# A float32 MLP's first product by seven half-size block products in place of eight, on one Trainium2 core

## Chip, cores and metric

The kernel runs on one core of a Trainium2 chip. The metric is the device time of one execution in microseconds (us). Engines: PE is TensorE (matmuls), DVE VectorE, ACT ScalarE, POOL GpSimd, SP SyncE, which issues most DMAs.

## The reference

Attention without a softmax, a norm, and two MLPs over 2304 tokens of 512 features, in float32:

```python
kv = np.einsum('bhsd,bhse->bhde', k, v)              # 4 batches, 8 heads, 576 x 64
out = np.einsum('bhsd,bhde->bhse', q, kv)
rms = np.sqrt(np.mean(out * out, axis=-1, keepdims=True) + 1e-06)
x = heads_side_by_side(out / rms * g_norm)           # 2304 x 512
# first MLP, w_in 512 x 2048
h = np.maximum(x @ w_in, 0.0); x = h * h @ w_out
# second MLP: 4 experts, w1[e] 512 x 1024, p = domain_probs / their sum
for e in range(4):
    h = np.maximum(x @ w1[e], 0.0)
    out2 += p[:, e:e + 1] * (h @ w2[e])
```

## The kernel before

Every float32 operand of a product is split into a high part in TensorE's reduced float32 format (`F32R`) and the rest in the same format; a product is three matmuls, high x low, low x high, high x high, added up in one bank of PSUM. `split` (L100) makes the parts: a copy on ACT gives the high part, a subtraction on POOL the low one.

Tokens are cut into blocks `BLK`, four of 512 and one of 256 (blocks 0 to 4). The inner features of the first MLP (2048) and of the second one (4 x 1024) are cut into slices of 256: slices 0 to 7 belong to the first MLP, 8 to 23 to the second. The kernel is a list of units, each a name that `run` (L348) turns into a call:

- `f<s>.<j>.<c>` is `g1` (L262): the first product of slice s for token block j and one of two feature chunks of 128, 4 inner chunks x 3 terms = 12 matmuls (L277) into one bank. In the first MLP ACT then takes ReLU and square and `split` the result. In the second ACT takes the ReLU into the high part `hh` (L285) and DVE makes the low part `hl` (L286).
- `g<s>.<j>.<c>` is `g2a` (L291), the second product of the first MLP: 2 x 3 matmuls (L301) for each of four output chunks, added to the accumulator `acc` on DVE (L308). After slice 7 the sum is split into `xh` and `xl`, the tokens of the second MLP.
- `h<s>.<j>.<t>` is `g2b` (L313), the second product of the second MLP: 2 x 3 matmuls (L323) for each tile of 128 tokens, scaled by the expert's weight and added to `acc` on DVE (L333). After the last slice the tile is stored.
- `w` is `split_w` (L138): the next quarter of a slice's weights is split, and a later quarter loaded into one of two `raw` buffers (L113). The weights of the first MLP come as float64 and are narrowed by six operations on DVE (L119 to L133).
- `k`, `o`, `c`, `b` are the attention: k^T v, q times that, norms, transposes. `p` works out the expert weights.

The list `RAMP` mixes the attention with slices 0 and 1; `rest` (L61) makes the order after it by rule: for each slice and block both `f` units, then the second products of the block before it, then a `w`. Each engine works through its instructions in order; the framework puts them in order at build time by the list, and a unit waits for a free buffer. Buffers that the change touches: eight banks of PSUM (`ps`), `tmp` (8 buffers of 2 KB per partition), weights in threes (`wp`), `hh` and `hl` in twos (`hp`), `xh` and `xl` as one tile each (`xp`).

Of the kernel before, what the change touches and what calls it, by code (L numbers as in the profile page):

```python
# [10 lines left out]
F32 = mybir.dt.float32  # L11
# [7 lines left out]
P = 128  # L19
# [39 lines left out]


def rest():  # L61
    def second(s, j):
        if s < NS1:
            return [f"g{s}.{j}.{c}" for c in range(KD)]
        return [f"h{s}.{j}.{t}" for t in range(BLK[j][1] // P)]

    r, prev = [], (1, NB - 1)
    for s in range(2, NS):
        for j in range(NB):
            r += [f"f{s}.{j}.{fc}" for fc in range(FC)] + second(*prev) + ["w"]  # L70
            prev = (s, j)
    return r + second(*prev)
# [3 lines left out]
def fused_kernel(ctx, tc, kvm, kvt, qt, g2, probs, w64, w32, out):  # L76
# [61 lines left out]
    def split_w():  # L138
        i = w_next[0]
        w_next[0] += 1  # L140
        s, c = divmod(i, 4)
        if s >= NS:
            return
        if c == 0:
            w_t[s] = [
                wp.tile([P, k, n], F32R, tag=t, name=f"{t}{s}")
                for t, k, n in (("ah", KD, FS), ("al", KD, FS), ("bh", FC, DM), ("bl", FC, DM))
            ]
        hi, lo = w_t[s][c // 2 * 2 : c // 2 * 2 + 2]
# [11 lines left out]
        load_w(i + 2)  # L161

# [1 line left out]
    kv_in, q_in, tails, stage, st_t, po_t, att_mid = {}, {}, {}, [None], {}, {}, {}  # L164
# [84 lines left out]
    def att_b(t):  # L249
        xn = att_mid.pop(t)  # L250
        pt = ps.tile([P, KD, P], F32, tag="ps", name=f"pt{t}")
        for c in range(KD):
            nc.tensor.transpose(pt[:, c, :], xn[:, c * P : (c + 1) * P], ident)  # L253
        dst = slice(t * P, (t + 1) * P)
        xg = tmp.tile([P, KD, P], F32, tag="tmp", name=f"xg{t}")
        nc.scalar.activation(out=xg, in_=pt, func=AF.Copy, scale=g_sb)
        split(xh[:, :, dst], xl[:, :, dst], xg)

# [1 line left out]
    h_t, acc_t = {}, {}  # L260

    def g1(s, j, fc):  # L262
        t0, n = BLK[j]
        ah, al = w_t[s][:2]
        if fc == 0:
            hh = hp.tile([P, FC, 512], F32R, tag="hh", name=f"hh{s}_{j}")
            hl = hp.tile([P, FC, 512], F32R, tag="hl", name=f"hl{s}_{j}")
            h_t[s, j] = (hh, hl)
        hh, hl = h_t[s, j]
        pt = ps.tile([P, 512], F32, tag="ps", name=f"p1_{s}_{j}_{fc}")  # L270
        fs = slice(fc * P, (fc + 1) * P)
        ts = slice(t0, t0 + n)
        steps = [
            (w[:, k, fs], x[:, k, ts]) for k in range(KD) for w, x in ((al, xh), (ah, xl), (ah, xh))
        ]
        for i, (w, x) in enumerate(steps):
            nc.tensor.matmul(pt[:, :n], w, x, start=(i == 0), stop=(i == len(steps) - 1))  # L277
        if s < NS1:
            r = tmp.tile([P, 512], F32, tag="tmp", name=f"r{s}_{j}_{fc}")
            nc.scalar.activation(out=r[:, :n], in_=pt[:, :n], func=AF.Relu)  # L280
            sq = tmp.tile([P, 512], F32, tag="tmp", name=f"s{s}_{j}_{fc}")
            nc.scalar.activation(out=sq[:, :n], in_=r[:, :n], func=AF.Square)
            split(hh[:, fc, :n], hl[:, fc, :n], sq[:, :n])
        else:
            nc.scalar.activation(out=hh[:, fc, :n], in_=pt[:, :n], func=AF.Relu)  # L285
            nc.vector.scalar_tensor_tensor(  # L286
                out=hl[:, fc, :n], in0=pt[:, :n], scalar=0.0, in1=hh[:, fc, :n].bitcast(F32),
                op0=ALU.max, op1=ALU.subtract,
            )

    def g2a(s, j, c):  # L291
        t0, n = BLK[j]
        bh, bl = w_t[s][2:]
        hh, hl = h_t[s, j]
# [13 lines left out]
        nc.vector.tensor_tensor(out=a, in0=pt[:, :n], in1=a, op=ALU.add)  # L308
        if s == NS1 - 1:
            ts = slice(t0, t0 + n)  # L310
            split(xh[:, c, ts], xl[:, c, ts], a)

    def g2b(s, j, i4):  # L313
# [32 lines left out]
    unit = dict(k=att_kv, o=att_a, c=att_c, b=att_b, w=split_w, p=probs_p, f=g1, g=g2a, h=g2b)  # L346

# [76 lines left out]
```

## Time and profile before

| | us |
|---|---|
| median of 3 runs | 1267.77 (1266.41 to 1270.11) |
| profiled execution, span from first to last instruction | 1264.5 |
| PE busy | 1242.0 (98%) |
| DVE busy | 613.8 (49%) |
| ACT busy | 327.6 (26%) |
| POOL busy | 318.9 (25%) |

The page of the profile gives busy times over the whole span; of the profiled execution it has no time but the span. Stretches of the span, waits and the chain of work that ended last are read from the trace, in us from the span's start. A matmul is pipelined, so the length of one is not the distance from one to the next.

### The profile page before, as it was taken

How to read it: one execution, taken by the hardware profiler on the slowest of the kernel's cores; microseconds unless marked ns; L12 is line 12 of the kernel's file. 1: busy time of each engine (PE TensorE's matmuls, PEld its weight loads, DVE VectorE, ACT ScalarE, POOL GpSimd, SP SyncE). 2: the span in 40 equal slices, each digit the busy share in tenths (PEclk: the TensorE clock that was granted, in tenths of full speed). 3: DMA queues.
4: the chain of work that ended last, by engine and by line, in shares of the span. 5: the costliest groups of instructions: out<-in, count | busy, mean ns of one | idle time of the engine just before them, and what ended most of it. 6: DMA issues, size and time to landing. Idle time of an engine off the chain costs nothing.

```text
span 1264.5 us, 14555 instructions
## 1 busy us (share of the span) xinstructions
PE 1242.0 (98%) x5960; PEld 1043.9 (83%) x5960; DVE 613.8 (49%) x897; ACT 327.6 (26%) x596; POOL 318.9 (25%) x260
## 2 busy tenths in 40 slices
PE   7999979999999999999999999999999999999998
PEld 6888768888888888888888888888888888888887
DVE  6977897877222223444344443444334433444434
ACT  3564334433434452111111111111111111110110
POOL 3566565644533471100101101001001001010000
PEclk9999989999999999999999999999999999999999
DMA  7701222111000100100001001001001000000003
GB/s 298 244 25 52 82 84 67 51 51 42 9 17 18 34 17 17 34 10 25 29 6 34 17 17 34 17 17 34 17 17 34 11 23 30 4 17 1 1 34 117
DMA packets 22243, 53.40 MB, mean 42 GB/s; under 512 B 2721, under 2 KB 2721, under 8 KB 22177
## 3 DMA queue, kind: packets, MB, share of 16 engines
q1 hardware_dynamic: 21888, 52.44, 12.1%
q8 instruction: 47, 0.77, 0.2%
q14 instruction: 20, 0.16, 0.0%
q10 hardware_dynamic: 288, 0.04, 0.0%
HBM read 47.75 MB, written 4.72 MB: 41 GB/s over the span
## 4 chain that ended last, share of the span: by engine, by line
PE 91%; DVE 6%; POOL 1%; issue 1%; ACT 1%; DMA 0%; POOLq 0%; ACTq 0%; DVEq 0%
PE p L277 44%; PE p L323 31%; PE p L301 13%; DVE k L133 1%; DVE u L128 1%; DVE u L123 1%; PE pk L195 1%; PE po L210 1%; DVE k L127 1%; DVE u L119 1%; DVE acc L308 1%; PE pt L253 0%; DVE st L220 0%; DVE k L132 0%; DMA kvs<-in_kvm 0%
## 5 line engine op out<-in xcount | busy, mean ns | idle before, releaser
L277 PE MATMUL p<-xh,al 128*128 128x512 f32 (+1 forms) x960 | 353.4, 368 | 0.0
L277 PE MATMUL p<-xl,ah 128*128 128x512 f32 (+1 forms) x960 | 353.3, 368 | 0.0
L277 PE MATMUL p<-xh,ah 128*128 128x512 f32 (+1 forms) x960 | 353.1, 368 | 0.0
L333 DVE SCALAR_TENSOR_TENSOR acc<-p,p_sb,acc 128x512 f32<-128x512 f32 x270 | 202.7, 751 | 143.3 <-PE p L323 140.9
L286 DVE SCALAR_TENSOR_TENSOR hl<-p,hh 128x512 fp32r<-128x512 f32 (+1 forms) x160 | 102.0, 637 | 317.1 <-ACT hh L285 317.1
L285 ACT ACTIVATE hh<-p 128x512 fp32r<-128x512 f32 (+1 forms) x160 | 88.6, 554 | 616.5 <-PE p L277 616.5
L323 PE MATMUL p<-bl,hh 128*128 128x512 f32 x576 | 224.3, 389 | 0.0
L323 PE MATMUL p<-bh,hl 128*128 128x512 f32 x576 | 224.3, 389 | 0.0
L323 PE MATMUL p<-bh,hh 128*128 128x512 f32 x576 | 224.1, 389 | 0.0
L277 PEld LDWEIGHTS p<-xh,al 128*128 128x128 f32 x960 | 181.0, 188 | 31.0 <-PE po L210 0.2
L277 PEld LDWEIGHTS p<-xl,ah 128*128 128x128 f32 x960 | 181.0, 189 | 30.7 <-POOL xl L102 0.2
L277 PEld LDWEIGHTS p<-xh,ah 128*128 128x128 f32 x960 | 180.9, 188 | 30.0
L308 DVE TENSOR_TENSOR acc<-p,acc 128x512 f32<-128x512 f32 (+1 forms) x140 | 88.0, 632 | 128.0 <-PE p L301 127.6
L102 POOL TENSOR_TENSOR al<-raw,ah 128x512 fp32r<-128x512 f32 x32 | 40.8, 1297 | 427.3 <-ACT ah L101 427.3
L102 POOL TENSOR_TENSOR hl<-s,hh 128x512 fp32r<-128x512 f32 (+1 forms) x80 | 100.0, 1254 | 146.3 <-ACT hh L101 125.2
L301 PE MATMUL p<-hl,bh 128*128 128x512 f32 (+1 forms) x320 | 120.0, 375 | 8.2 <-POOL hl L102 8.2
L323 PEld LDWEIGHTS p<-bh,hh 128*128 128x128 f32 x576 | 108.1, 188 | 22.6
L323 PEld LDWEIGHTS p<-bl,hh 128*128 128x128 f32 x576 | 108.2, 188 | 22.0
L323 PEld LDWEIGHTS p<-bh,hl 128*128 128x128 f32 x576 | 108.2, 188 | 21.8
L301 PE MATMUL p<-hh,bl 128*128 128x512 f32 (+1 forms) x320 | 119.5, 374 | 2.0 <-ACT hh L101 1.9
L301 PE MATMUL p<-hh,bh 128*128 128x512 f32 (+1 forms) x320 | 119.1, 372 | 0.0
L280 ACT ACTIVATE r<-p 128x512 f32<-128x512 f32 (+1 forms) x80 | 44.0, 550 | 139.2 <-PE p L277 133.5
(62 smaller groups left out, 919.3 us busy)
## 6 DMA issues: line engine op xcount, KB each, us to landing
raw<-in_w SPq DMA_DIRECT2D x32, 512.0 KB, 3.8
raw<-in_w SPq DMA_DIRECT2D x64, 256.0 KB, 3.0
kvm<-in_kvm SPq DMA_DIRECT2D x10, 512.0 KB, 3.8
q<-in_qt SPq DMA_DIRECT2D x18, 256.0 KB, 4.5
out<-acc SPq DMA_DIRECT2D x18, 256.0 KB, 2.0
kvs<-in_kvm SPq DMA_DIRECT2D x6, 512.0 KB, 7.3
kvt<-in_kvt SPq DMA_DIRECT2D x4, 256.0 KB, 6.1
p_raw<-in_probs ACTq DMA_DIRECT2D x1, 36.0 KB, 5.1
```

What stands on the lines that cost most here:

```text
L102: nc.gpsimd.tensor_tensor(out=lo, in0=full, in1=hi.bitcast(F32), op=ALU.subtract)
L119: nc.vector.tensor_scalar(out=u, in0=high, scalar1=3, scalar2=0x3FFFFFF8, op0=ALU.logical_shift_left, op1=ALU.bitwise_and,)
L123: nc.vector.scalar_tensor_tensor(out=u, in0=high, scalar=0xC0000000, in1=u, op0=ALU.bitwise_and, op1=ALU.bitwise_or)
L127: nc.vector.tensor_scalar(out=k, in0=high, scalar1=0x7FFFFFFF, scalar2=None, op0=ALU.bitwise_and)
L277: nc.tensor.matmul(pt[:, :n], w, x, start=(i == 0), stop=(i == len(steps) - 1))
L280: nc.scalar.activation(out=r[:, :n], in_=pt[:, :n], func=AF.Relu)
L285: nc.scalar.activation(out=hh[:, fc, :n], in_=pt[:, :n], func=AF.Relu)
L286: nc.vector.scalar_tensor_tensor(out=hl[:, fc, :n], in0=pt[:, :n], scalar=0.0, in1=hh[:, fc, :n].bitcast(F32), op0=ALU.max, op1=ALU.subtract,)
L301: nc.tensor.matmul(pt[:, :n], w, h, start=(i == 0), stop=(i == len(steps) - 1))
L308: nc.vector.tensor_tensor(out=a, in0=pt[:, :n], in1=a, op=ALU.add)
L323: nc.tensor.matmul(pt, h, w, start=(i == 0), stop=(i == len(steps) - 1))
L333: nc.vector.scalar_tensor_tensor(out=a, in0=pt, scalar=pe, in1=a, op0=ALU.mult, op1=ALU.add)
```

## The change

In the second MLP the first product of two token blocks of 512 is taken as one product of 2 x 2 blocks: the weights of a slice, 512 x 256, are four blocks a11, a21, a12, a22 of 256 x 128, and the tokens four blocks b11 to b22 of 256 x 512. Seven block products and sums before and after them (Winograd's form of Strassen's algorithm) give what eight gave.

- Sums of weights: s1 to s4, on DVE (`operands`), once per slice; then splits of the four blocks and the four sums.
- Sums of tokens: t1 to t4, on DVE, for the pair (0, 1) ahead of the second MLP and for the pair (2, 3) ahead of the second group (units `x<g>.<i>`, function `right`). Four buffers `o` in the place of the x tiles hold the parts of all seven right operands: b11 and t2, t1 and t3, b21 and b22, t4.
- Products: units `s<v>.<b>.<i>`, i from 0 to 6, 6 matmuls each, into four banks a to d; products 4, 5 and 6 add into a bank that already holds a product. ACT copies one bank (p1), DVE adds u2, u4 and three more sums, and ReLU and `hl` follow as before.
- Two groups: all sixteen slices for blocks 0, 1 and 4, then all sixteen again for blocks 2 and 3. So the second MLP's weights are loaded and split twice; a pass of a slice has a number v, 8 to 39. Block 4 keeps its old products.
- Order: `merge` puts the second products of the blocks before between the seven products.
- Buffers: the x tiles by block, both parts of a weight in one tile, constants of the attention in its own pool, and a pool `ext` in the attention's place after `RAMP` with a third pair of h buffers and the second weight operand. A load of the second MLP's weights brings two quarters (512 KB).

```diff
+GRP2 = (((0, 1), (4,)), ((2, 3),))
 def rest():
...
+    for v in range(2, NS1):
         for j in range(NB):
...
+            if v == NS1 - 1 and j >= 2:
+                r += [f"x0.{j - 2}"]
+    for g, group in enumerate(GRP2):
+        for v in range(NS1 + g * NS2, NS1 + (g + 1) * NS2):
+            for blk in group:
+                b = blk[0]
+                if v == NS1 and b == 0:
+                    r += second(*prev) + ["x0.3"]
+                    prev = (v, ())
...
+                if v == NS1 + NS2:
+                    r += [f"x1.{i}" for i in range(4)]
+                if len(blk) == 2:
+                    units = [f"s{v}.{b}.{i}" for i in range(7)]
+                else:
+                    units = [f"f{v}.{b}.{fc}" for fc in range(FC)]
+                r += ["w"] * (blk == group[0]) + merge(units, second(*prev)) + ["w"] * (blk == group[-1])
+                prev = (v, blk)
...
+    def operands(i, v):
...
+        nc.vector.tensor_tensor(out=s1, in0=a21, in1=a22, op=ALU.add)
+        nc.vector.tensor_tensor(out=s2, in0=s1, in1=a11, op=ALU.subtract)
+        nc.vector.tensor_tensor(out=s3, in0=a11, in1=a21, op=ALU.subtract)
+        nc.vector.tensor_tensor(out=s4, in0=a12, in1=s2, op=ALU.subtract)
+        for n, a in enumerate(w_t[v]):
+            split(*(a[:, x, 0:2].rearrange("p o k f -> p (o k) f") for x in range(2)), r[:, :, n * P : (n + 1) * P])
+            split(*(a[:, x, 2:4] for x in range(2)), st[n])
...
+    OPS = (("b11", "t2"), ("t1", "t3"), ("b21", "b22"), ("t4",))
...
+        o = xp.tile([P, 2, 4, 512], F32R, tag="xs", name=f"o{g}_{i}", bufs=4)
+        for m, name in enumerate(OPS[i]):
+            o_t[pair[0], name] = (o, m * 2)
+            for k in range(2):
+                hi, lo = o[:, 0, m * 2 + k, :], o[:, 1, m * 2 + k, :]
+                if name[0] == "b":
+                    split(hi, lo, x_part(pair, name, k))
+                    continue
+                full = t_sum(pair, name, k)
+                nc.scalar.activation(out=hi, in_=full, func=AF.Copy)
+                nc.vector.tensor_tensor(out=lo, in0=full, in1=hi.bitcast(F32), op=ALU.subtract)
...
+    def t_sum(pair, name, k):
...
+        if name == "t3":
+            return sub("t3", b22, b12)
+        t1 = sub("t1", b12, b11)
+        if name == "t1":
+            return t1
+        t2 = sub("t2", b22, t1)
+        return t2 if name == "t2" else sub("t4", b21, t2)
...
+    PRODUCTS = (
+        (0, 0, "b11", "a", False), (0, 3, "t2", "b", False), (0, 2, "t1", "c", False),
+        (1, 2, "t3", "d", False), (1, 3, "b22", "c", True), (0, 1, "b21", "a", True),
+        (1, 1, "t4", "d", True),
+    )
...
+    def g1s(v, b, i):
...
+        steps = [
+            (w[:, x, op, k, :], o[:, y, k0 + k, :]) for k in range(2) for x, y in ((1, 0), (0, 1), (0, 0))
+        ]
...
+        if i == 0:
+            nc.scalar.activation(out=new("p1"), in_=pa, func=AF.Copy)
+        elif i == 1:
+            nc.vector.tensor_tensor(out=new("u2"), in0=pb, in1=su["p1"], op=ALU.add)
+        elif i == 2:
+            nc.vector.tensor_tensor(out=new("u4"), in0=pc, in1=su["u2"], op=ALU.add)
+        elif i == 3:
...
+            nc.vector.tensor_tensor(out=pb, in0=pd, in1=su["u4"], op=ALU.add)
+            relu(v, j2, 1, pb)
+        elif i == 4:
+            nc.vector.tensor_tensor(out=pc, in0=pc, in1=su["u2"], op=ALU.add)
+            relu(v, j2, 0, pc)
+        elif i == 5:
+            relu(v, j1, 0, pa)
+        else:
+            nc.vector.tensor_tensor(out=pd, in0=pd, in1=su["u2"], op=ALU.add)
+            relu(v, j1, 1, pd)
```

The order that `rest` gives, around the start of the second MLP, in a pass of the first group, and in one of the second:

```
f7.2.0 f7.2.1 g7.1.0 .. g7.1.3 x0.0 f7.3.0 f7.3.1 g7.2.0 .. g7.2.3 x0.1 f7.4.0 f7.4.1 g7.3.0 .. g7.3.3 x0.2
g7.4.0 .. g7.4.3 x0.3 w s8.0.0 .. s8.0.6 x0.4 f8.4.0 h8.1.0 .. h8.1.3 f8.4.1 h8.0.0 .. h8.0.3 w
w s9.0.0 s9.0.1 s9.0.2 s9.0.3 h8.4.0 s9.0.4 s9.0.5 s9.0.6 h8.4.1 f9.4.0 h9.1.0 .. h9.1.3 f9.4.1 h9.0.0 .. h9.0.3 w
w w s25.2.0 h24.3.0 s25.2.1 h24.3.1 s25.2.2 h24.3.2 s25.2.3 h24.3.3 s25.2.4 h24.2.0 s25.2.5 h24.2.1 s25.2.6 h24.2.2 h24.2.3
```

## Rows read from the trace of the kernel before

**Rows 1.** The page, busy us of each engine (share) and instructions.
```profile
PE 1242.0 (98%) x5960; PEld 1043.9 (83%) x5960; DVE 613.8 (49%) x897; ACT 327.6 (26%) x596; POOL 318.9 (25%) x260
```
**Rows 2.** Busy time by stretch; the header names the columns.
```profile
core 0: us, PE busy (x) PEld busy (x) DVE busy (x) ACT busy (x) POOL busy (x), PEclk, DMA share, GB/s
160.00:200.00 40.00, 34.99 (x155) 28.79 (x156) 39.62 (x47) 16.40 (x30) 27.37 (x21) 0.91 0.25 80
200.00:240.00 40.00, 40.00 (x201) 34.07 (x200) 31.95 (x43) 17.02 (x30) 22.18 (x17) 1.00 0.18 58
420.00:480.00 60.00, 60.00 (x300) 51.15 (x299) 16.96 (x29) 31.91 (x56) 38.51 (x34) 1.00 0.08 27
480.00:1260.00 780.00, 780.00 (x3622) 653.55 (x3621) 315.16 (x446) 117.49 (x214) 70.70 (x57) 1.00 0.07 23
```
**Rows 3.** Waits of PE in the whole span: us in total, times, longest.
```profile
PE p L301 <- POOL hl L102: 8.2, 5, 3.2
PE pk L195 <- DMA kvs<-in_kvm: 5.3, 2, 5.1
PE p L301 <- ACT hh L101: 1.9, 2, 1.3
```
**Rows 4.** Chain of work in the second MLP: start us, us, what, matmuls.
```profile
954.74 2.87 PE p L277 x24
957.61 5.47 PE p L323 x24
963.08 5.44 PE p L277 x24
...
976.68 5.44 PE p L323 x24
```
**Rows 5.** Groups by line and shape, PE: count | busy us, mean ns.
```profile
L277 PE MATMUL p<-xh,al 128*128 128x512 f32 x768 | 299.2, 390 | 0.0
L323 PE MATMUL p<-bl,hh 128*128 128x512 f32 x576 | 224.3, 389 | 0.0
```
**Rows 6.** Groups by line and shape, DVE, ACT, POOL; last, line 128's min/median/max.
```profile
L333 DVE SCALAR_TENSOR_TENSOR acc<-p,p_sb,acc 128x512 f32<-128x512 f32 x270 | 202.7, 751 | 143.3 <-PE p L323 140.9
L286 DVE SCALAR_TENSOR_TENSOR hl<-p,hh 128x512 fp32r<-128x512 f32 x128 | 88.5, 692 | 296.5 <-ACT hh L285 296.5
L285 ACT ACTIVATE hh<-p 128x512 fp32r<-128x512 f32 x128 | 76.5, 598 | 512.9 <-PE p L277 512.9
L308 DVE TENSOR_TENSOR acc<-p,acc 128x512 f32<-128x512 f32 x112 | 76.5, 686 | 107.1 <-PE p L301 106.9
L102 POOL TENSOR_TENSOR al<-raw,ah 128x512 fp32r<-128x512 f32 x32 | 40.8, 1297 | 427.3 <-ACT ah L101 427.3
L128 DVE SCALAR_TENSOR_TENSOR u<-k,u 128x512 f32<-128x512 uint32 x32 | 30.7, 959 | 0.3
L101 ACT ACTIVATE ah<-raw 128x512 fp32r<-128x512 f32 x32 | 18.5, 624 | 14.3 <-PE p L277 14.2
L286 DVE SCALAR_TENSOR_TENSOR hl<-p,hh 128x256 fp32r<-128x256 f32 x32 | 13.5, 420 | 20.6 <-ACT hh L285 20.6
L308 DVE TENSOR_TENSOR acc<-p,acc 128x256 f32<-128x256 f32 x28 | 11.5, 419 | 20.8 <-PE p L301 20.8
...
L128 DVE SCALAR_TENSOR_TENSOR u<-k,u x32: 674/693/1693, 11.2 to 314.7; 128x512 f32<-128x512 uint32 x32
```
**Rows 7.** DVE and POOL in order of time: start us, us, engine, line.
```profile
293.50 0.68 DVE L128 SCALAR_TENSOR_TENSOR u<-k,u 128x512 f32<-128x512 uint32 x1
294.10 0.68 DVE L308 TENSOR_TENSOR acc<-p,acc 128x512 f32<-128x512 f32 x1
294.70 0.41 DVE L132 TENSOR_SCALAR k<-u 128x512 uint32<-128x512 uint32 x1
...
301.13 1.69 DVE L128 SCALAR_TENSOR_TENSOR u<-k,u 128x512 f32<-128x512 uint32 x1
...
300.98 1.30 POOL L102 TENSOR_TENSOR hl<-s,hh 128x512 fp32r<-128x512 f32 x1 [1.43 <-ACT hh L101]
```
**Rows 8.** DMA issues of the page: count, KB each, median us to landing.
```profile
raw<-in_w SPq DMA_DIRECT2D x32, 512.0 KB, 3.8
raw<-in_w SPq DMA_DIRECT2D x64, 256.0 KB, 3.0
...
out<-acc SPq DMA_DIRECT2D x18, 256.0 KB, 2.0
```
**Rows 9.** DVE in order of time, its last instruction.
```profile
1260.67 0.75 DVE L333 SCALAR_TENSOR_TENSOR acc<-p,p_sb,acc 128x512 f32<-128x512 f32 x1 [0.61 <-PE p L323]
```

More of the change, by code (lines that the diff above doesn't have):

```diff
@@ L253, in att_b @@
             nc.tensor.transpose(pt[:, c, :], xn[:, c * P : (c + 1) * P], ident)
-        dst = slice(t * P, (t + 1) * P)
+        x = x_t[t // 4]
+        dst = slice(t % 4 * P, (t % 4 + 1) * P)
         xg = tmp.tile([P, KD, P], F32, tag="tmp", name=f"xg{t}")
         nc.scalar.activation(out=xg, in_=pt, func=AF.Copy, scale=g_sb)
-        split(xh[:, :, dst], xl[:, :, dst], xg)
+        split(x[:, 0, :, dst], x[:, 1, :, dst], xg)
     h_t, acc_t = {}, {}
-    def g1(s, j, fc):
[L263 to L269, printed above, removed]
-        pt = ps.tile([P, 512], F32, tag="ps", name=f"p1_{s}_{j}_{fc}")
[L271 to L275, printed above, removed]
+    n_h = [0]
@@ new lines, in new_h, with left @@
+    def new_h(v, j):
+        pool, more = (ext, "3") if ext is not None and n_h[0] % 3 == 2 else (hp, "")
+        n_h[0] += 1
+        h_t[v, j] = [
+            pool.tile([P, FC, 512], F32R, tag=t + more, name=f"{t}{v}_{j}") for t in ("hh", "hl")
+        ]
+        return h_t[v, j]
+    def g1(s, j, fc):
+        n = BLK[j][1]
+        x = x_t[j]
+        hh, hl = new_h(s, j) if fc == 0 else h_t[s, j]
+        pt = ps.tile([P, 512], F32, tag="ps", name=f"p1_{s}_{j}_{fc}")
+        def left(part, k):
+            if s < NS1:
+                return w_t[s][0][:, part, k, fc * P : (fc + 1) * P]
+            return w_t[s][fc][:, part, k // 2, k % 2, :]
+        steps = [(left(a, k), x[:, b, k, :]) for k in range(KD) for a, b in ((1, 0), (0, 1), (0, 0))]
@@ L276, in g1 @@
         for i, (w, x) in enumerate(steps):
             nc.tensor.matmul(pt[:, :n], w, x, start=(i == 0), stop=(i == len(steps) - 1))
[L278 to L289, printed above, removed]
+        if s >= NS1:
+            relu(s, j, fc, pt[:, :n])
+            return
@@ L308, in g2a, with x_part, right @@
         nc.vector.tensor_tensor(out=a, in0=pt[:, :n], in1=a, op=ALU.add)
[L309 to L313, printed above, removed]
+    OPS = (("b11", "t2"), ("t1", "t3"), ("b21", "b22"), ("t4",))
+    PLACE = {n: (i, k) for i, names in enumerate(OPS) for k, n in enumerate(names)}
+    o_t, t_tmp = {}, {}
+    def x_part(pair, name, k):
+        return acc_t[pair[int(name[2]) - 1]][:, (int(name[1]) - 1) * 2 + k, :]
+    def right(g, i):
+        pair, *alone = GRP2[g]
+        if i == 4:
+            (j,) = alone[0]
+            x_t[j] = xp.tile([P, 2, KD, BLK[j][1]], F32R, tag="xt", name=f"xb{j}", bufs=1)
+            for k in range(0, KD, 2):
+                split(*(x_t[j][:, a, k : k + 2, :] for a in range(2)), acc_t[j][:, k : k + 2, :])
+            return
+        o = xp.tile([P, 2, 4, 512], F32R, tag="xs", name=f"o{g}_{i}", bufs=4)
[9 more added lines that the diff above has]
+                nc.vector.tensor_tensor(out=lo, in0=full, in1=hi.bitcast(F32), op=ALU.subtract)
@@ new lines, in t_sum, with sub @@
+    def t_sum(pair, name, k):
+        b11, b12, b21, b22 = (x_part(pair, f"b{x}", k) for x in ("11", "12", "21", "22"))
+        def sub(m, a, b):
+            t = tmp.tile([P, 512], F32, tag="tmp", name=f"{m}_{name}_{pair[0]}_{k}")
+            nc.vector.tensor_tensor(out=t, in0=a, in1=b, op=ALU.subtract)
+            return t
+        if name == "t3":
[5 more added lines that the diff above has]
+        return t2 if name == "t2" else sub("t4", b21, t2)
@@ new lines, in fused_kernel, with new @@
+    PRODUCTS = (
+        (0, 0, "b11", "a", False), (0, 3, "t2", "b", False), (0, 2, "t1", "c", False),
+        (1, 2, "t3", "d", False), (1, 3, "b22", "c", True), (0, 1, "b21", "a", True),
+        (1, 1, "t4", "d", True),
+    )
+    pr, su = {}, {}
+    def g1s(v, b, i):
+        j1, j2 = b, b + 1
+        place, op, name, bank, more = PRODUCTS[i]
+        w = w_t[v][place]
+        o, k0 = o_t[b, name]
+        if not more:
+            pr[bank] = ps.tile([P, 512], F32, tag="ps", name=f"p{bank}{v}_{b}")
+        steps = [
+            (w[:, x, op, k, :], o[:, y, k0 + k, :]) for k in range(2) for x, y in ((1, 0), (0, 1), (0, 0))
+        ]
+        for m, (x, y) in enumerate(steps):
+            nc.tensor.matmul(
+                pr[bank], x, y, start=(m == 0 and not more), stop=(m == len(steps) - 1),
+                skip_group_check=more,
+            )
+        pa, pb, pc, pd = (pr.get(x) for x in "abcd")
+        def new(m):
+            su[m] = tmp.tile([P, 512], F32, tag="tmp", name=f"{m}_{v}_{b}")
+            return su[m]
+        if i == 0:
[5 more added lines that the diff above has]
+        elif i == 3:
+            new_h(v, j2)
+            new_h(v, j1)
+            nc.vector.tensor_tensor(out=pb, in0=pd, in1=su["u4"], op=ALU.add)
[5 more added lines that the diff above has]
+            relu(v, j1, 0, pa)
+        else:
+            nc.vector.tensor_tensor(out=pd, in0=pd, in1=su["u2"], op=ALU.add)
+            relu(v, j1, 1, pd)
@@ L344, in probs_p @@
         )
-    unit = dict(k=att_kv, o=att_a, c=att_c, b=att_b, w=split_w, p=probs_p, f=g1, g=g2a, h=g2b)
+    unit = dict(
+        k=att_kv, o=att_a, c=att_c, b=att_b, w=split_w, p=probs_p, f=g1, g=g2a, x=right, s=g1s, h=g2b
+    )
+    ext = None
     def run(name):
@@ L353, in fused_kernel @@
         small = actx.enter_context(tc.tile_pool(name="small", bufs=3))
+        g_sb = small.tile([P, 1], F32, name="g_sb", bufs=1)
+        ident = small.tile([P, P], F32, name="ident", bufs=1)
+        kvd += [small.tile([P, P], F32, name=f"kvd{i}", bufs=1) for i in range(NKVD)]
         make_identity(nc, ident)
```

134 lines of the change are left out of this document (92 added, 42 removed).

## Prediction, made before the changed kernel was run

> **What bounds the kernel now.** I read the busy shares first, then the busy time by stretch, then the waits of TensorE (PE), then the chain of work. The shares put PE at 1242.0 of 1264.5 us and VectorE (DVE) at 613.8 [rows 1]; that is an average, so the stretches matter. From 200 us on PE is busy for the whole of each stretch, 780.00 of 780 us from 480 to 1260, while DVE is busy for 315.16, ScalarE (ACT) for 117.49 and GpSimd (POOL) for 70.70 of them, at a granted clock of 1.00, the 2.4 GHz level [rows 2]. PE idles 1264.5 - 1242.0 = 22.5 us; 3.8 of it is the end behind the last accumulation at 1260.67 [rows 9], and some 18.6 lie before 200 us, where PE's longest waits are for hl, for a k/v load and for hh [rows 3]. From 160 to 200 DVE is busy 39.62 of 40 us and PE only 34.99, at a clock of 0.91 [rows 2]: the start is held by DVE, the second MLP by PE alone.
>
> A busy PE can still be a slow one, so I take its rate from the chain: 24 matmuls of 512 columns take 5.44 us, 226.7 ns each, on line 277 as on line 323, and 24 of 256 columns 2.87 us, 119.6 ns each [rows 4]. The 390 ns in the groups by line [rows 5] is the length of one matmul, which overlaps the next; it must not be multiplied by a count. A slice of the second MLP is four blocks of 5.44 and one of 2.87 on line 277 and 4.5 of 5.44 on line 323, 49.1 us; sixteen slices are 786 us, the length of the stretch. So a matmul removed in the second MLP is worth 226.7 ns, as long as nothing else becomes late.
>
> **What the change removes.** Line 277 ran 96 matmuls of 512 columns per slice (4 blocks x 2 feature chunks x 4 inner chunks x 3 terms; 768 x 3 over 24 slices [rows 5]). A pair of blocks takes seven products of 2 x 3 = 6 now, 42 instead of 48. Two pairs, sixteen slices: 32 x 6 = 192 matmuls fewer, 192 x 226.7 ns = 43.5 us. Block 4 and the second products keep their counts. PE per slice becomes 9.52 + 2.87 + 60 x 0.2267 = 26.0 us in the first group (blocks 0, 1, 4) and 9.52 + 48 x 0.2267 = 20.4 us in the second, 46.4 for 49.1.
>
> The Trainium skill (TensorE: Matmul & The Clock Gate, Back-to-back issue gap) puts a sustained stream of weight load and matmul at about 131 ns for 512 columns; by it the 192 would be worth 25.2 us. The chain has 226.7 ns in every slice, so the rule does not hold here, and the sum goes by the row.
>
> **What it adds in the steady slices.** Per pair and slice DVE gets five adds of a bank and a buffer. Their nearest row is the add of line 308, 686 ns at 512 columns [rows 6]; back to back, the next operation starts 0.60 us after such a one [rows 7]. It also gets four sums of weights at 256 columns: 419 ns (line 308 at 256 [rows 6]), or that plus a wait for POOL (below). What stays is hl at 692 ns (420 for block 4) and the accumulation at 751 [rows 6]. First group, per 26.0 us of PE: 5 x 0.69 + 4 x 0.42 + 4 x 0.69 + 2 x 0.42 + 10 x 0.75 = 16.2 us, 62%. Second, per 20.4 us: 3.4 + 1.7 + 2.8 + 8 x 0.75 = 13.9 us, 68%. DVE was at 315 of 780, 40%; it still isn't full. ACT has one copy and six splits at 0.62 and four to six ReLUs at 0.60 per slice, POOL six splits at 1.30 = 7.8 us of 20.4 [rows 6]. Neither is near PE.
>
> What counts is one wait that is new: product 4 (counted from 0) adds into the bank of product 2, so its first matmul waits until DVE has read that bank for u4, and every matmul behind it in PE's queue waits too. Between the end of product 2 and the start of product 4 stand product 3 (1.36 us) and one second-product tile (1.36 us): 2.72 us for an add of 0.69, so DVE may be 2 us late at no cost. In the very first slice no tile stands there, and it is 1.36. Products 5 and 6 add into banks read two to four units earlier. A pair holds four banks; four are left for tiles that need one for 1.36 + 0.75 us. I count both at nothing; the cover is DVE's 32 to 38% of idle time.
>
> **The price that the trace shows beforehand: DVE against POOL.** Line 128 reads two buffers in SBUF; it takes 674 ns at best and 959 on average [rows 6], while POOL is busy a little over half of the time [rows 2]. At 301.13 one took 1.69 us: POOL had begun an operation of 1.30 at 300.98, and the DVE one ended 0.54 us after it; at 293.50, with POOL idle, it took 0.68 [rows 7]. So an operation on two buffers waits out POOL's, and all new sums of weights and of tokens are of that kind. At 512 columns such a sum costs 0.69 (no POOL) to 0.69 + 1.3; I take 0.69 + 0.27, from the mean of line 128. The Trainium skill (SBUF — State Buffer, Who interferes with whom) states it as an exclusive lock, held for a whole instruction, when DVE has two SBUF inputs; the trace agrees (1.69 against 0.68 us), and it speaks against putting these sums on DVE beside POOL's splits. In steady slices 4 x 0.27 = 1.1 us falls at the slice's start, ahead of u2 and u4, inside the 2 us above. I allow 0.8 us in all for slices where it doesn't fit; the bounds are 0 and 0.5 us in each of 32 pairs, 16 us.
>
> **The two changes of operands.** Before each group the token sums are made: on DVE 6 operations for t2, 4 each for t1 and t3, 8 for t4, 22 in all, 15.2 us (13.2 back to back); on ACT 14 copies, 8.8 us; on POOL 6 subtractions, 7.8 us.
> Change A, into the second MLP: the sums can start when block 1 is complete. PE still has f7.3, g7.2, f7.4, g7.3, g7.4 then: 3 x 5.44 + 2 x 2.87 = 22.1 us, and t4 is needed only 8.2 us after that. DVE owes 12 accumulations there (8 x 0.69 + 4 x 0.42 = 7.2 us), then three adds and a split: 22 + 3 = 25 us of 30, plus 22 x 0.27 = 6. Just full. Bounds 0 and 6 us; I take 1.
> Change B, between the groups: the four operand buffers come free one by one as the last pair of slice 23 runs. From its product 1 to product 3 of the next pair, PE has 27.4 us of work. DVE owes 15.1 + 1.2 of its own (all back to back: adds 3.1, hl 3.2, 11 accumulations 7.3, weights 1.5, the new u2 and u4 1.2) and 8.5 for t2, t1 and t3: 24.8 us, plus 18 waits for POOL of 0.27 = 5. That is 2 us over; t4 adds 4.9 in the next 5. Bounds 0 and 10 us; I take 3.
>
> **Edits at nothing.** The second MLP's weights are loaded and split twice: 64 loads of 512 KB at 3.8 us instead of 64 of 256 KB at 3.0 [rows 8], two per 20 to 26 us and a slice ahead. The first group's ten stores now stand in the middle of SP's queue, each behind its accumulation, with loads behind them; the slice of lead covers that. The end keeps its form: the last accumulation, then a store of 2.0 us [rows 8, 9]. The third h buffer and the x tiles by block only loosen waits; the order of the start may shift either way (bounds -3 and +3 around its 18.6 us); I take 0.
>
> **The rivals.**
> 1. Forecast. Span 1264.5 - 43.5 + 0.8 + 1 + 3 = 1225.8. The page gives no time of that execution but its span; the median of the runs, 1267.77, is 3.3 above it, so 1229. Own range 1221 (no stall, start 3 shorter) to 1237. For it: PE is full in all of the second MLP, and DVE keeps a third.
> 2. DVE against POOL decides at both changes and in some slices: 6 + 10 + 5 us given back, 1267.8 - 43.5 + 21 = 1245. For it: 1.69 against 0.68. Against: POOL's 7.8 us per slice leave most of it free.
> 3. Slower: product 4 waits for u4 in every pair. At 43.5 / 32 = 1.36 us per pair the gain is gone; that needs DVE 3.4 us late each time, as when all four weight sums wait out an operation of POOL (5.2 us) right in front of u2. All 5.2 late gives 3.2 us per pair, 1327; 2 us per pair, the middle of that case, gives 1288. Against: the sums run at a slice's start, three products earlier.
> 4. The removed matmuls are worth less than the spacing, since pairs run slower: 42 in 10.1 us instead of 9.52 gives back 18.3, 1247. Against: one rate on both lines, and a change of line costs 0.03 us (5.47 against 5.44 [rows 4]). This is the time that the page's 131 ns would give.
>
> **Chances.** Forecast 0.75, rival 2 0.15, rival 3 0.05 with another 0.03 at no change, rival 4 0.02. The range 1221 to 1246 takes in 1 and most of 2. A measurement of this kernel tells some 0.3% (3.8 us) from no change. Faster 0.92, within 0.3% 0.03, slower 0.05.
>
> **What would show it.** In the chain, 42 matmuls of 9.52 us per pair; PE busy throughout the second MLP but for gaps of 1 to 5 us at its first pair and between the groups; waits of PE for u4 under 5 us in sum; token sums near 0.96 us on average. Wrong, if PE waits for DVE in every slice, if a product takes more than 1.36 us, or if the first 200 us change by more than 3.

## The result, and the profile after

The changed kernel takes 1235.58 us (median of 4 runs, 1235.17 to 1238.97) against 1267.32: a ratio of 0.975, 95% interval 0.9732 to 0.9767, 31.7 us less. The prediction was 1229.0 us, 38.8 less than the 1267.77 known then, with a range of 1221 to 1246.

The page has PE still at 98%, busy for 35.5 us less, and DVE at 64% where it was at 49% [rows 1]. It also shows the loads of weights, to set beside [rows 8]:

```profile
PE 1206.5 (98%) x5768; PEld 1012.0 (82%) x5768; DVE 797.5 (64%) x1229; ACT 427.3 (35%) x766; POOL 486.0 (39%) x382
...
raw<-in_w SPq DMA_DIRECT2D x96, 512.0 KB, 3.7
```

Busy time by stretch, with the columns of [rows 2]. The stretches are the start, the first MLP, the change to the second one, the first group, the change between the groups, the second group:

```profile
core 0: us, PE busy (x) PEld busy (x) DVE busy (x) ACT busy (x) POOL busy (x), PEclk, DMA share, GB/s
0.00:200.00 200.00, 180.23 (x950) 151.47 (x951) 163.12 (x257) 89.53 (x172) 110.98 (x94) 0.97 0.37 127
200.00:460.00 260.00, 260.00 (x1261) 220.09 (x1260) 131.94 (x194) 106.56 (x185) 116.89 (x92) 1.00 0.11 35
460.00:500.00 40.00, 37.56 (x199) 32.04 (x198) 34.28 (x48) 18.76 (x38) 21.26 (x15) 1.00 0.04 14
500.00:870.00 370.00, 370.00 (x1790) 312.80 (x1789) 221.84 (x355) 102.07 (x184) 110.73 (x86) 1.00 0.12 42
870.00:930.00 60.00, 55.37 (x239) 44.71 (x238) 53.14 (x76) 22.90 (x41) 27.67 (x19) 0.94 0.23 79
930.00:1220.00 290.00, 290.00 (x1281) 240.15 (x1280) 184.61 (x292) 86.85 (x148) 98.50 (x76) 1.00 0.13 44
```

In both groups PE is busy for the whole of the stretch, 370.00 of 370 and 290.00 of 290 us, with DVE at 60 and 64%. In the chain a product of six matmuls takes 1.36 us, 226.7 ns each as in [rows 4], and product 4 (into bank c) follows its tile with no gap:

```profile
530.96 1.36 PE pa L467 x6
532.32 1.36 PE pb L467 x6
533.68 1.36 PE pc L467 x6
535.04 1.36 PE pd L467 x6
536.40 1.36 PE p L512 x6
537.76 1.36 PE pc L467 x6
```

What was lost lies at the two changes of operands. At the first, PE idles 40 - 37.56 = 2.4 us, at the second 60 - 55.37 = 4.6, and there the granted clock averages 0.94. In the stretches of 3 us further down it is 0.56, 0.50 and 0.80: with two levels, 1.00 and 0.50, that is 6.8 us at half speed, worth 3.4 us of matmuls at most. The profiled execution was also 3.4 us longer than the other three, for a reason at its start (below).

The second change in detail. PE in order of time (start us, us, engine, line, what was waited for):

```profile
895.36 1.52 PE L467 MATMUL pa<-o,a 128*128 128x512 f32 x6
...
899.44 1.48 PE L467 MATMUL pd<-o,a 128*128 128x512 f32 x4
901.64 0.73 PE L467 MATMUL pd<-o,a 128*128 128x512 f32 x2 [0.73 <-DVE o L429]
...
905.50 1.42 PE L467 MATMUL pa<-o,a 128*128 128x512 f32 x5 [1.75 <-ACT p L478]
908.95 2.93 PE L467 MATMUL pc<-o,a 128*128 128x512 f32 x6 [2.02 <-DVE u L482]
```

DVE beside it; line 437 makes token sums, 429 their low parts, 480 is u2, 482 is u4:

```profile
902.17 0.67 DVE L437 TENSOR_TENSOR t_t<-acc,acc 128x512 f32<-128x512 f32 x1
902.88 1.42 DVE L437 TENSOR_TENSOR t_t<-acc,t_t 128x512 f32<-128x512 f32 x2
904.22 0.69 DVE L437 TENSOR_TENSOR t_t<-acc,acc 128x512 f32<-128x512 f32 x1
905.01 0.69 DVE L437 TENSOR_TENSOR t_t<-acc,t_t 128x512 f32<-128x512 f32 x1
905.62 0.69 DVE L429 TENSOR_TENSOR o<-t_t,o 128x512 fp32r<-128x512 f32 x1
906.22 0.69 DVE L437 TENSOR_TENSOR t_t<-acc,t_t 128x512 f32<-128x512 f32 x1
906.82 0.69 DVE L480 TENSOR_TENSOR u<-pb,p 128x512 f32<-128x512 f32 x1
907.60 0.69 DVE L429 TENSOR_TENSOR o<-t_t,o 128x512 fp32r<-128x512 f32 x1
908.21 0.68 DVE L482 TENSOR_TENSOR u<-pc,u 128x512 f32<-128x512 f32 x1
```

And ACT, whose copy p1 (line 478) stands behind a copy for t4 that itself waits for DVE:

```profile
904.34 0.63 ACT L428 ACTIVATE o<-t_t 128x512 fp32r<-128x512 f32 x1 [7.18 <-DVE t_t L437]
904.87 0.58 ACT L478 ACTIVATE p<-pa 128x512 f32<-128x512 f32 x1
```

The operands of product 0 were ready in time. u4, which product 4 needs, is ready only at 908.9, because the operations for t4, which only product 6 needs, stand ahead: on DVE seven of the eight ahead of u2 and all eight ahead of u4, and on ACT t4's first copy ahead of p1. The gap of 1.75 us has the same cause: PE's order has five matmuls of product 5 ahead of product 4 here, and product 5 adds into bank a, so it waits until p1, the copy of that bank, is made. The 0.73 us at 901.64 are another matter: there product 3 waits for a low part of its own operand, t3. Right behind the two long gaps six matmuls take 2.93 us from the first one's start to the last one's end, where they took 1.52 at 895.36, and the granted clock of the stretches shows why:

```profile
905.00:908.00 3.00, 1.42 (x5) 0.86 (x5) 2.90 (x5) 1.08 (x2) 0.00 (x0) 1.00 0.13 48
908.00:911.00 3.00, 2.05 (x5) 1.67 (x6) 2.48 (x5) 0.60 (x1) 0.00 (x0) 0.56 0.19 73
911.00:914.00 3.00, 3.00 (x9) 2.32 (x8) 2.09 (x4) 1.09 (x2) 0.00 (x0) 0.50 0.04 14
914.00:917.00 3.00, 3.00 (x13) 2.35 (x12) 1.60 (x3) 1.14 (x2) 1.30 (x1) 0.80 0.00 0
```

0.50 is the 1.2 GHz level. So the theories to be told apart were: the order in the queues of DVE and ACT (Q), the amount of DVE's work in the window (D, the working of the prediction), the lock between DVE and POOL (K), and the change of groups itself, its buffers and stores (B).

### The profile page after: what moved, and what is told of

It is laid out like the page before. It is cut to its first block, busy times and chain, and to the rows that moved or that the text cites. A ratio compares the mean times of both kernels' runs of the same rounds, so it can differ in the third digit from the quotient of the medians.

```text
span 1237.2 us, 14956 instructions
## 1 busy us (share of the span) xinstructions
PE 1206.5 (98%) x5768; PEld 1012.0 (82%) x5768; DVE 797.5 (64%) x1229; ACT 427.3 (35%) x766; POOL 486.0 (39%) x382
## 4 chain that ended last, share of the span: by engine, by line
PE 87%; DVE 10%; issue 1%; POOL 1%; DMA 1%; ACT 1%; DVEq 0%; ACTq 0%; POOLq 0%
PE p L512 31%; PE p L369 17%; PE p L390 12%; PE pc L467 7%; PE pd L467 7%; PE pa L467 7%; PE pb L467 3%; DVE t_t L437 2%; PE po L293 1%; PE pk L278 1%; DVE acc L397 1%; DVE o L429 1%; DVE k L185 1%; DVE u L175 1%; DVE k L179 1%
## 5 line engine op out<-in xcount | busy, mean ns | idle before, releaser
L512 PE MATMUL p<-b,hh 128*128 128x512 f32 x1152 | 382.7, 390 | 0.0
L512 PEld LDWEIGHTS p<-b,hh 128*128 128x128 f32 x1152 | 216.6, 188 | 44.5
L512 PE MATMUL p<-b,hl 128*128 128x512 f32 x576 | 224.5, 390 | 0.0
L369 PE MATMUL p<-x,a 128*128 128x512 f32 (+1 forms) x960 | 205.1, 369 | 0.0
L390 PE MATMUL p<-hh,b 128*128 128x512 f32 (+1 forms) x640 | 192.4, 374 | 3.0 <-ACT hh L146 2.9
L369 PEld LDWEIGHTS p<-x,a 128*128 128x128 f32 x960 | 168.1, 189 | 30.8 <-POOL x L147 0.2
L390 PEld LDWEIGHTS p<-hh,b 128*128 128x128 f32 x640 | 118.2, 191 | 24.2 <-ACT hh L146 3.4
L390 PE MATMUL p<-hl,b 128*128 128x512 f32 (+1 forms) x320 | 120.3, 376 | 7.6 <-POOL hl L147 7.6
L512 PEld LDWEIGHTS p<-b,hl 128*128 128x128 f32 x576 | 108.4, 188 | 21.3
L467 PE MATMUL pd<-o,a 128*128 128x512 f32 x384 | 99.2, 393 | 0.9 <-DVE o L429 0.7
```

The lines of the kernel that those rows point to most:

```text
L390: nc.tensor.matmul(pt[:, :n], w, h, start=(i == 0), stop=(i == len(steps) - 1))
L467: nc.tensor.matmul(pr[bank], x, y, start=(m == 0 and not more), stop=(m == len(steps) - 1), skip_group_check=more,)
```

## The experiments

All edits are against the changed kernel. PE's idle time in the two stretches and the granted clock come from the same view as above, for each run:

| run | us | ratio, interval | idle at change 1 | at change 2 | clock 1, 2 |
|---|---|---|---|---|---|
| changed kernel | 1235.58 | 0.9732 to 0.9767 | 2.4 | 4.6 | 1.00, 0.94 |
| again | 1236.54 | 0.9729 to 0.9764 | 2.4 | 4.6 | 0.96, 0.97 |
| t4_later | 1228.30 | 0.9667 to 0.9707 | 0.1 | 2.1 | 1.00, 1.00 |
| sums_kept | 1232.46 | 0.9698 to 0.9737 | 0.0 | 4.5 | 1.00, 0.97 |
| lows_on_pool | 1238.95 | 0.9747 to 0.9784 | 4.4 | 3.2 | 0.91, 0.97 |
| kept_later | 1229.62 | 0.9684 to 0.9713 | 0.0 | 2.5 | 1.00, 0.97 |
| kept_later_w | 1225.60 | 0.9653 to 0.9685 | 0.0 | 0.6 | 1.00, 1.00 |
| later_w | 1227.75 | 0.9658 to 0.9703 | 0.1 | 1.0 | 1.00, 1.00 |
| second_plain | 1251.18 | 0.9854 to 0.9884 | 2.4 | 0.3 | 0.96, 1.00 |
| no_tile_between | 1238.67 | 0.9752 to 0.9784 | 2.4 | 5.5 | 0.96, 0.97 |
| weight_sums_twice | 1238.88 | 0.9747 to 0.9781 | 2.5 | 4.1 | 0.96, 0.94 |
| weight_sums_four | 1244.29 | 0.9784 to 0.9834 | 2.5 | 7.6 | 0.96, 0.93 |

(Stretches 460 to 500 and 870 to 930 us; second_plain from 860, weight_sums_four to 940.)

**again.** The same kernel.

> The changed kernel once more, nothing edited. In its first profile PE starts the first product of the first MLP 4.8 us later than in the kernel before (51.9 against 47.1 us), with the same order of matmuls, and the executions that were not profiled are 3.4 us shorter. Theory C (the late start is this one execution's loads): the new profile has that product near 47 to 49 us, a span near 1233.6, a time of 1235.5. Theory L (the new layout delays the start): 51.9 again. Under both, the matmuls behind 480 us lose the same as before: about 2.7 us at the first pair of the second MLP and about 8.9 between the groups (4.6 us idle and 4.2 at the lower clock).

This execution, of 1234.94 us, had a span of 1233.2, 4.0 less than the first, and the start was the whole of it. The first 200 us of the kernel before, and then of this run:

```profile
0.00:200.00 200.00, 181.40 (x968) 152.56 (x969) 165.95 (x261) 91.10 (x175) 112.67 (x96) 0.97 0.37 127
...
0.00:200.00 200.00, 181.48 (x968) 152.54 (x969) 165.71 (x261) 91.13 (x175) 112.62 (x96) 0.97 0.37 127
```

Both have 968 matmuls behind them at 200 us; the first profile of the changed kernel had 950, 18 x 0.2267 = 4.1 us behind. So the new layout does not delay the start, and theory L is out. But the loads of theory C are not the reason either: PE starts its first matmul at 5.08 us in the first profile and at 5.03 in this one. The two part a little later. The same stretch in the first profile, and then in this one:

```profile
11.00:17.00 6.00, 6.00 (x25) 5.10 (x24) 2.44 (x6) 1.06 (x3) 2.83 (x2) 1.00 1.05 403
...
11.00:17.00 6.00, 5.81 (x41) 5.13 (x40) 3.17 (x8) 2.26 (x5) 2.83 (x2) 1.00 1.05 401
```

PE is busy in both, but gets through 25 matmuls in one and 41 in the other; the column of the clock, 1.00 in both, does not show why. The starts of the twelve profiles in the table vary by some 4 us (950 to 968 matmuls at 200 us), and the runs of the kernel before spread as far (1266.4 to 1270.9), so a difference of 1 or 2 us between two runs is read from the stretches behind 200 us. From this pair of profiles the account is clean: 1264.5 - 1233.2 = 31.3 us of 43.5. Of the 12.2 us lost, 2.4 + 4.6 are PE's idle time at the changes and (0.04 x 40) + (0.03 x 60) = 3.4 the lower clock; 1.8 us are not in these views. Some 0.7 of them is a matter of counting, by an estimate from [rows 4] and [rows 5]: idle time starts at a matmul's end, 0.39 us after its start, where the next one would have started after 0.227, so each of the four waits is 0.16 us longer than its idle time.

**t4_later.** Order alone:

```diff
-                    r += second(*prev) + ["x0.3"]
+                    r += second(*prev)
...
-                    r += [f"x1.{i}" for i in range(4)]
+                    r += [f"x1.{i}" for i in range(3)]
...
+                    if v == NS1 + g * NS2:
+                        units.insert(4, f"x{g}.3")
```

> Order alone: the units that make t4 (8 DVE operations, 2 copies on ACT) move behind product 3 of the pair that needs them, at both changes; no work is added or removed. Theory Q (in the queues of DVE and ACT the t4 sums stand ahead of u2, u4 and p1, so product 4 waits for t4 that only product 6 needs): product 4 no longer waits, product 6 waits for what is left; loss at the first pair 2.7 to 0 or 1 us, between the groups 8.9 to 3 or 5, time 1229 to 1231. Theory D (the sum of DVE's work in the window sets it): the wait only moves from product 4 to product 6, time 1233 to 1236.

8.2 us less than `again` with not one operation fewer, a little more than Q forecast: the idle time falls from 2.4 to 0.1 and from 4.6 to 2.1 us, and the clock stays at 1.00. D, which moved the wait without shortening it, is out as the only cause. The two stretches:

```profile
460.00:500.00 40.00, 39.95 (x210) 34.15 (x209) 32.20 (x49) 17.36 (x34) 22.50 (x17) 1.00 0.08 27
870.00:930.00 60.00, 57.90 (x262) 46.80 (x261) 55.96 (x82) 25.79 (x47) 30.59 (x22) 1.00 0.26 88
```

Of the 2.1 us that stay, 0.7 are product 3's wait for t3's low part, as before, and 1.2 product 6's wait for t4.

**sums_kept.** Fewer sums, old order:

```diff
-            t = tmp.tile([P, 512], F32, tag="tmp", name=f"{m}_{name}_{pair[0]}_{k}")
-            nc.vector.tensor_tensor(out=t, in0=a, in1=b, op=ALU.subtract)
-            return t
+            if (m, pair, k) not in t_tmp:
+                t = tmp.tile([P, 512], F32, tag="tmp", name=f"{m}_{name}_{pair[0]}_{k}")
+                nc.vector.tensor_tensor(out=t, in0=a, in1=b, op=ALU.subtract)
+                t_tmp[m, pair, k] = t
+            return t_tmp[m, pair, k]
```

> t1 and t2 are kept in their buffers and used again, so the token sums of a change are 16 operations on DVE instead of 22; order, buffers of the operands, ACT and POOL as in the changed kernel. A sum has cost 0.98 us on average. Theory D (DVE's work in the window sets it): 6 x 0.98 = 5.9 us less in front of product 4, so the loss at the first pair goes to 0, between the groups the idle 4.6 goes to 0 or 1 and the clock does not fall, 10 to 11 us gained, time 1225 to 1227. Rival B (the operand buffers come free too late): nothing changes, 1235.5.

Neither number: 1232.5. The first change is free of loss, as D has it; there either edit, this one or t4_later, is enough. At the second PE idles 4.5 us as before, though DVE was busy only 48 of the 60 us: another wait has come to the front. ACT, then POOL, then SP's queue:

```profile
881.50 0.63 ACT L428 ACTIVATE o<-t_t 128x512 fp32r<-128x512 f32 x1 [0.31 <-DVE t_t L438]
892.17 0.63 ACT L146 ACTIVATE a<-raw 128x512 fp32r<-128x512 f32 x1 [10.04 <-DMA raw<-in_w]
...
877.90 6.42 POOL L147 TENSOR_TENSOR o<-acc,o 128x512 fp32r<-128x512 f32 x4 [5.17 <-ACT o L146]
884.29 3.45 POOL L147 TENSOR_TENSOR b<-raw,b 128x512 fp32r<-128x512 f32 x2
...
860.59 27.50 SPq L165 DMA_DIRECT2D raw<-in_w  x2
```

ACT's next instruction is the split of a following slice's weights. They are loaded late: the load waits for a buffer that POOL frees at 887.7, after it has worked through four operand parts. For 10 us the token copies and p1 behind it in ACT's queue don't run, ready or not. (The edit also holds four of the eight `tmp` buffers until t4 is made; no run tells that apart.)

**lows_on_pool.** Low parts of the token sums on POOL:

```diff
-                full = t_sum(pair, name, k)
-                nc.scalar.activation(out=hi, in_=full, func=AF.Copy)
-                nc.vector.tensor_tensor(out=lo, in0=full, in1=hi.bitcast(F32), op=ALU.subtract)
+                split(hi, lo, t_sum(pair, name, k))
```

> The low parts of t1 to t4 are made by POOL in place of DVE: 14 token sums on DVE instead of 22, 8 more subtractions of 1.3 us on POOL per change. Theory D (DVE's count of operations sets it): 8 x 0.98 = 7.8 us less on DVE, time 1226 to 1229. Rival K (the lock between DVE and POOL sets it: the sums wait out POOL's operations, and the port, not DVE, is full): POOL's 10.4 us more are in the way of the 14 sums that remain, and the loss stays within 3 us of the 11.6 or grows, time 1233 to 1238.

About the time that rival K gave: 8 operations fewer on DVE gain nothing, 1239.0 us. The waits change their name (PE now waits for POOL, 4.3 us for hl at the first change and 3.2 for operands at the second) and not their sum (7.5 us, and 7.0 in `again`). POOL is no place to put this work. K's mechanism is not shown by it, though: the 28 sums left on DVE do take longer, 1.10 us on average against 0.96 for the same lines in `again`, but what PE waits for is POOL's own work, with POOL busy 29.8 of 40 us at the first change (21.9 in `again`).

**kept_later, kept_later_w, later_w.** Both edits; both and the weights' unit moved; the two moves without the kept sums. The move of the weights' unit, by which both units of slice 25's weights come behind product 3 and each later unit of the second group one place later:

```diff
+                if v == NS1 + NS2 - 1:
+                    two = False
+                if v == NS1 + NS2:
+                    units.insert(5, "w")
+                    one = False
```

> t1 and t2 kept (16 sums in place of 22) and the t4 units behind product 3, both at once. Theory Q2 (what stands in front of u2, u4 and p1 in the queues of DVE and ACT decides, the number of sums only where nothing else is in front): loss at the first pair 0, between the groups 2 to 4 us, what the split of slice 25's weights on ACT leaves; time 1226 to 1229. Theory D (DVE's work decides): the gains of 8 and 4 us add up to the whole loss, 1224 to 1225.

> As kept_later, and the first unit of slice 25's weights behind product 3 of the first pair of the second group in place of ahead of it. With t1 and t2 kept ACT waited 10 us for those weights to load, with the token copies and p1 behind it in its queue. Theory Q2: that wait no longer stands in front of anything, PE idles under 1 us between the groups and keeps its clock, time 1224 to 1226. Theory D: no difference from kept_later within 1 us.

> Order alone, at both places: the t4 units and the first unit of slice 25's weights behind product 3; all 22 token sums stay. Theory Q2 (the order in the queues decides): between 1225 and 1228, PE idle under 2 us behind 480 us. Theory D (the number of sums decides): 6 x 0.98 = 5.9 us more than kept_later_w between the groups, 1230 to 1232.

kept_later gains nothing over t4_later (1229.6 and 1228.3, the intervals overlap), just above Q2's range and 4.6 us above D's: ACT waits 10.0 us for the load again. With that unit moved behind product 3 it is 1225.6, PE's idle time 0.6 us and the clock 1.00 throughout, as Q2 has it; D saw no more than 1 us of difference here. later_w, with all 22 sums, is at 1227.8, idle 1.0: within Q2's bounds and not the 5.9 us more that D asked for. So order takes some 8.8 of the 10.9 us between `again` and kept_later_w (8.2 with the t4 units alone); the six sums take the other 2.2 at most, which the intervals of the two runs do not clearly separate. kept_later_w beats the changed kernel by 10.0 us: 42.2 us under the kernel before in the medians of its own comparison (1267.78), of 43.5.

**second_plain.** The seven products in the first group alone:

```diff
-GRP2 = (((0, 1), (4,)), ((2, 3),))
+GRP2 = (((0, 1), (4,)), ((2,), (3,)))
...
+        if g == 1:
+            x = x_t[2 + i] = xp.tile([P, 2, KD, 512], F32R, tag="xs", name=f"xb{2 + i}", bufs=4)
+            for k in range(KD):
+                split(x[:, 0, k, :], x[:, 1, k, :], acc_t[2 + i][:, k, :])
+            return
```

> One part alone: the first group keeps its seven products, the second group (blocks 2 and 3) takes its first products the old way, from plain parts of the tokens; passes, loads of weights and their sums stay. 16 pairs lose 6 matmuls instead of 32: 96 x 226.7 ns = 21.8 us of PE back. Theory O (the loss between the groups comes from the token sums and from what stands in queue around them): that loss of 7 to 9 us is gone, time 1235.6 + 21.8 - 8 = 1249. Rival B (the change of groups itself costs it: operand buffers, the stores, the weights of the next pass): the loss stays, 1257.

1251.2, 2 us over O and 6 under B. With no token sums at the second change its idle time is 0.3 us, though the stores and the second loads are as they were. Of the four operand buffers only two are filled there, so for the buffers the better evidence is later_w: it fills all four and idles 1.0 us. ACT waits 15 us for weights there too, in front of nothing that is urgent.

**no_tile_between.** Half of the cover of product 4 taken away:

```diff
+                both = merge(units, second(*prev))
+                if len(blk) == 2:
+                    both.remove(units[4])
+                    both.insert(both.index(units[3]) + 1, units[4])
```

> The tile of a second product that stood between product 3 and product 4 of every pair now stands behind product 4; nothing else moves. Between the end of product 2 and the start of product 4 PE has 1.36 us instead of 2.72 for an add u4 of 0.69. If the cover was as counted (DVE at most 2 us late, mostly not late at all): 0 to 0.3 us lost per pair, 1236 to 1245, nearest 1238. If DVE was near the edge already (the sums of weights and the accumulations in front of u4): 1 us and more per pair, 1267 or more.

1238.7, 2.1 us over `again` with overlapping intervals; 0.9 of it is idle time at the second change (5.5 us for 4.6). In both groups PE is busy for all of 370.00 and 290.00 us. The 1.36 us of the expectation hold in the first group alone. In the second one a tile stands behind product 2 as well, so 2.72 us are left there, and the changed kernel has 4.08. The narrow case, a pair of the first group (product 2, 3 and 4; then u2, u4 and a sum of weights on DVE):

```profile
558.50 1.52 PE L471 MATMUL pc<-o,a 128*128 128x512 f32 x6
559.86 1.52 PE L471 MATMUL pd<-o,a 128*128 128x512 f32 x6
561.22 1.52 PE L471 MATMUL pc<-o,a 128*128 128x512 f32 x6
...
558.77 0.69 DVE L484 TENSOR_TENSOR u<-pb,p 128x512 f32<-128x512 f32 x1 [2.04 <-PE pb L471]
560.12 0.69 DVE L486 TENSOR_TENSOR u<-pc,u 128x512 f32<-128x512 f32 x1 [0.66 <-PE pc L471]
560.73 0.41 DVE L242 TENSOR_TENSOR w<-raw 128x256 f32<-128x256 f32 x1
```

u4 begins 0.1 us after product 2's last matmul (560.02) and is done at 560.81, 0.4 us ahead of product 4's start at 561.22. DVE is not late at all, and the sums of weights stand behind u4 in its order, not ahead of it.

**weight_sums_twice, weight_sums_four.** The four sums of weights in a loop of two, and of four:

```diff
+        for _ in range(4):
+            nc.vector.tensor_tensor(out=s1, in0=a21, in1=a22, op=ALU.add)
```

> In the changed kernel each of the four weight sums s1 to s4 is done twice: 4 x 0.47 = 1.9 us more on DVE per pass of a slice, right at its start, ahead of u2 and u4. If the cover is as counted (some 30% of DVE's time free, 2 us before product 4 waits): the steady slices lose nothing, at most 1 or 2 us more at the two changes, 1235 to 1239. If the sums in front of u4 were near the edge: up to 1.9 us in each of 32 pairs, 1250 or more.

> The weight sums done four times: 12 x 0.47 = 5.6 us more on DVE per pass. Second group: 13.9 + 5.6 = 19.5 us of 20.4 on DVE, 96%; first group 21.8 of 26.0. If DVE's idle time is the cover: PE starts to wait for DVE in the second group's passes, a few tenths to 1 us in each of 16, more at the changes, 1240 to 1255. If order and not DVE's fill decides in steady slices too: 3 us late in front of u4 in every pair, 1270 or more.

Twice over it takes 1238.9 us, inside the first expectation's range, and PE is busy for all of 370.00 and 290.00 us. Four times over (two executions) 1244.3 lies in the range of the second expectation, but not for its reason: DVE is at 77 and 90% in the two groups and PE still idles nowhere in them:

```profile
500.00:870.00 370.00, 370.00 (x1790) 312.82 (x1789) 286.33 (x522) 98.06 (x183) 111.84 (x87) 1.00 0.12 42
870.00:940.00 70.00, 62.42 (x259) 49.20 (x258) 64.82 (x104) 24.13 (x44) 31.65 (x19) 0.93 0.20 68
940.00:1220.00 280.00, 280.00 (x1237) 231.64 (x1236) 251.29 (x438) 84.04 (x144) 102.50 (x77) 1.00 0.13 46
```

Of the 7.7 us that it costs over `again`, 3.0 are idle time at the second change (7.6 for 4.6), where DVE is busy 64.82 of 70 us, and some 3 the lower clock there (0.07 x 70 against 0.03 x 60). The runs test less than both expectations say, since the sums stand behind u4 and not ahead of it. Only in the first passes of the second group does DVE run late. In one of them u4 begins 3.3 us after product 2's last matmul (968.79) and is done at 972.73, just ahead of product 4:

```profile
972.05 0.68 DVE L483 TENSOR_TENSOR u<-pc,u 128x512 f32<-128x512 f32 x1
...
972.78 1.43 PE L468 MATMUL pc<-o,a 128*128 128x512 f32 x5
```

## Why the prediction held, and where it missed

1. **192 matmuls at 226.7 ns.** Held. A product takes 1.36 us in the chain; kept_later_w, where little else is lost, has a span of 1222.9, 41.6 us under [rows 1]'s 1264.5. Rival 4, a lower worth, is out.
2. **Steady slices at (nearly) nothing.** Held; the 0.8 us allowed were 0. DVE's share, forecast at 62 and 68% from single durations, is 60 and 64%, since operations back to back start every 0.60 us [rows 7]. Rival 3 is out: even with DVE at 90% PE idles nowhere in the groups. The reason given was in part wrong, and that it did no harm was luck: the sums of weights, which I had ahead of u2 and u4, stand behind u4 (560.73 after 560.12 above), and the cover in the second group is 4.08 us, not 2.72.
3. **A sum against POOL.** Held in size: the 44 token sums of the changed kernel average 0.98 us (43 us in all) against the 0.96 taken from line 128 [rows 6], the longest 1.8. The Trainium skill (SBUF — State Buffer, Who interferes with whom) has a DVE instruction with two SBUF inputs contend with GpSimd's reads, under an exclusive lock; the trace agrees, with 0.98 us on average against 0.67 at best. In lows_on_pool, work moved from DVE to POOL gained nothing (1239.0 us).
4. **Change A: 1 us, change B: 3 us.** Mis-sized: 2.4 and 4.6 us of idle time, 8.0 at B with the lower clock in the first profile. The step that failed is "t4 is needed only 8.2 us after that", and the sum of DVE's work made with it. It counted what PE needs and when, as if each engine took its work by need. DVE and ACT take theirs in order, and the list has t4 ahead of product 0, so u2, u4 and p1 waited for it. t4_later, with the same work, gets 8.2 us back. The Trainium skill (TensorE: Matmul & The Clock Gate, Architectural detail) calls the queues of ScalarE and VectorE strictly first in, first out; the trace agrees, with p1 at 904.87 right behind a copy that had waited 7.18 us.
5. **The lower clock.** Missing from the sum altogether: 3.4 us, over a quarter of the 12.2 us lost. [Rows 2] had shown it, 0.91 in the stretch where PE was busy 34.99 of 40 us, and I did not carry it over to the gaps that I priced.
6. **Loads "a slice ahead".** True in the changed kernel as the list stands, and the second thing in line: once the sums were fewer, ACT stood 10.0 us in front of a load that waited for POOL. Naming the queue behind each moved unit, ACT's too, might have shown it.
7. **The 3.3 us around the span.** An execution is 1.8 us longer than its span (1238.97 and 1237.2); the rest was the profiled execution of before being some 1.5 us under the median. The forecast was made against the median, so this shifts nothing by itself.
8. **A sign of being wrong that came up.** The first 200 us changed by more than 3: by 4.1 in the first profile. `again` has the 968 matmuls of the kernel before, so it was that execution and not the layout.

In sum: the span forecast was 1225.8 us and that of `again` 1233.2, 7.4 more. A's idle time gives 1.4 of it, B's 1.6, the clock 3.4 and what these views don't show 1.8, less the 0.8 allowed for the steady slices.

## What to carry to other kernels

When an engine's products get shorter, its gain is what the others can be late, so price each moved or added unit by what stands behind it in the queue of every engine that it uses, not by when its result is needed. Work needed last should be issued last; here moving the two t4 units alone was worth 8.2 us, taking away 6 of 22 sums alone 4.1. And a gap of PE can cost more than its length: matmuls ran at the lower level behind some of the gaps here, though not behind all.

## What the runs showed of the hardware

- The same gap of 2.4 us, at the same place, left the granted clock at 1.00 in one execution (460 to 500 us, first profile) and took it to 0.96 in another (`again`). What decides between the two is not shown by these runs.
- Between two executions of one program the time at which PE has a given matmul behind it differed by 4.1 us at 200 us, with the same order of instructions. The two part between 11 and 17 us, where PE, busy in both, gets through 25 matmuls in one and 41 in the other; what decides that stays open.
- A single operation of DVE on two buffers in SBUF, 0.67 us alone, took up to 1.8 us beside POOL, and did so however the work was divided between the two.
